# Float64 weight words without a clamp, the split of w_out in the first up stage, and output stores on SyncE's queue, in a RetNet and SwiGLU kernel

## The chip, the cores and the metric

The kernel runs on one core of one Trainium2 chip. The metric is the device time in microseconds (us); lower is better. The engines are named PE (TensorE), ACT (ScalarE), DVE (VectorE), POOL (GpSimd) and SP (SyncE, which only issues transfers here).

## The reference

Retention over 4 sequences of 768 tokens with 8 heads of 64, then a gated feed-forward block on the 3072 x 512 result.

```python
for t in range(S):
    state = gamma * state + outer(k[t], v[t])      # per batch and head, 64 x 64
    y[t] = (1 / sqrt(D)) * q[t] @ state
x = y as (3072, 512)
g = x @ w_gate                                      # 512 x 1536
out = (g * sigmoid(g) * (x @ w_val)) @ w_out        # 1536 x 512
```

q, k and v are float32. The three weight matrices arrive as float64; the kernel gets them as 64-bit words and makes float32 of them itself.

## The kernel before, in words

**Segments.** The 24 chunks of 128 tokens are worked in four segments (NSEG) of six chunks, three each of two sequences. A segment has an attention part, an *up stage* (gate and value products for 12 slices of 128 columns of d_ff, f = 0 to 11) and a *down stage* (out += h[f] @ w_out[f], six token blocks in six PSUM banks). The attention of the next segment is woven into a down stage.

**The first segment is different.** Its up stage (`up`, L591) uses float32 products, seven per f (a seven-product scheme for the 2 x 2 blocks of x and the weights, `product` L599, matmul at L601, 28 matmuls per f). Later segments (`up3`, L769) use three passes of rounded parts per product (matmul at L765), and every down stage does so too (`down`, L829, matmul at L832). The parts are made by `near_a/b/c` (L657 to L664) and `far_a/b/c/d` (L666 to L676): a rounded leading part on ACT, a remainder on DVE or POOL, and a combination; `far` has a fourth operation, a scaling on ACT.

**Weights in the first up stage.** A *piece* is one slice f of gate and value ("up", 128 x 1024 words) or of w_out ("down", 128 x 512 words). Pieces 0 to 11 are up, 12 to 23 are down. A piece is loaded as raw 64-bit words (`load_piece`, letters U and D), and converted:
- `convert_a` on ACT: part a takes the absolute value of the high words as float (L219), part b copies the high words into a PSUM bank to keep the sign (L223), part c scales the low words and adds an offset (L226).
- `convert_b` on DVE: letter B clamps to a minimum and maximum (L236) and shifts left by 3 (L238), letter S takes the sign bit out of the PSUM copy and puts it in (L242), in parts of 512.
- `convert_c` on POOL (letter C, L252) adds the two as integers.

An up piece then gets three sums on DVE (`sums_t`, letter T, L266 through L80) and is stored in DRAM (`w_up`) for the later segments. A down piece is stored as plain float32 (`w_dn`, L203).

**The split of w_out** is in segment 0's down stage (`w_load`, L807): each slice is loaded from `w_dn` into chunk_x, split in three (`far_a` ACT L667, `far_b` POOL L670, `far_c` DVE L673, `far_d` ACT L676) into a tile `oitem` (three slots), used, and stored to `w_dn3`. Later segments only load `w_dn3`, 8.0 ahead of the use in the planner's time.

**What sets the order.** Each engine works in the order of issue. In the first up stage the order is written out: `aside(f, place)` runs the letters in the table `beside[f, place]` between the products of a step, place 0 to 5; in the text such a place is also counted as q = 6 f + place. Transfers to DRAM wait in `stores` until two places later. Everything else is put in a list of events with a due time in us of an assumed plan (`at`, L121), and `run` issues those due. In the plan a step of the first up stage takes UP0 = 9.45 and starts from T0 = 18. All loads, and the stores of weights, are issued from SP. `up` copies the first product of a step to `p1` on ACT (L620) before the bank is used again; `up3` does so with L781, which is issued through the helper line L122.

**The end of a down stage.** `finish` (L836) brings a bank out with ACT (even blocks, L845) or DVE (odd blocks, L843) into chunk_x, and issues the store of the output from ACT (L846).

**Side tables.** `load_side` brings turned decay tables for the later segments over the tables of the prologue, and `load_pair` loads k, q, v of the next segment; in the first up stage both come near the end.

Of the kernel before, what the change touches and what calls it, by code (L numbers as in the profile page):

```python
# [49 lines left out]
def tile_retnet_swiglu(  # L50
# [42 lines left out]
    spare = [place(f"spare{i}", 3 * DM, tag=f"o{i}") for i in range(3)]  # L93
# [61 lines left out]
    w_dn = [kept.tile([P, DM], F32, name=f"wdn{f}", tag=f"wdn{f}") for f in range(NF)]  # L155
# [16 lines left out]
    def load_piece(piece):  # L172
# [24 lines left out]
        if not wide and kind == "down":  # L197
            keep_dn(piece)

    def keep_dn(piece):  # L200
        kind, a = piece
        if kind == "down":
            nc.sync.dma_start(out=w_dn[a], in_=made[a % 5])  # L203
# [9 lines left out]

    def convert_a(piece, own, part=None):

        if piece in raw:
            d, lo, hi = words_of(piece)
            if part in (0, None):
                nc.scalar.activation(d, hi.bitcast(F32), AF.Abs)  # L219
            if part in (1, None):  # L220
                signs[piece] = []
                for i, o in enumerate(own):
                    nc.scalar.copy(banks[o], hi[:, ts(i, 512)].bitcast(F32))  # L223
                    signs[piece].append(banks[o])
            if part in (2, None):
                nc.scalar.activation(lo.bitcast(F32), lo, AF.Copy, scale=2.0 ** -51,  # L226
                                     bias=2.0)

    def convert_b(piece, part=None):


        if piece in raw:
            d = words_of(piece)[0]
            u = d.bitcast(U32)
            if part in (0, None):
                nc.vector.tensor_scalar(d, d, 122879.9921875, 2.0 ** -15, op0=ALU.min,  # L236
                                        op1=ALU.max)
                nc.vector.tensor_scalar(u, u, 3, None, op0=ALU.logical_shift_left)  # L238
            if part in (1, None):
                for i, t in enumerate(signs.pop(piece)):  # L240
                    v = u[:, ts(i, 512)]
                    nc.vector.scalar_tensor_tensor(v, t.bitcast(U32), 0x80000000, v,  # L242
                                                   op0=ALU.bitwise_and,
                                                   op1=ALU.bitwise_xor)


    def convert_c(piece, halves=1):
        if piece in raw:
# [6 lines left out]
            stores.append((places[0], lambda: keep_dn(piece)))  # L255
# [14 lines left out]
    pieces = [("up", f) for f in range(NF)] + [("down", f) for f in range(NF)]  # L270
# [767 lines left out]
```

## Time and profile before

| what | value |
|---|---|
| runs | 705.17, 706.85, 814.71 us; median 706.85 |
| profiled run | 704.16 us, span of instructions 702.4 us, mean granted clock 0.989 |
| PE, DVE, ACT, POOL busy | 95%, 71%, 56%, 35% of the span |
| data moved | 140.8 MB, mean 200 GB/s |
| first product of the first up stage to first down matmul | 29.69 to 145.26 us |
| down stage 0, first matmul to the first of segment 1's up stage | 145.26 to 230.72 us |
| the same for segment 1 and segment 2 | 321.09 to 391.88, 484.54 to 555.47 us |
| last down stage to the end | 648.9 to 702.4 us |

Times of operations are from one profiled execution. A group's mean is the length of one instruction; two of them on ACT or DVE that follow each other start about 0.1 us less than that apart. The busy time of PE counts overlapping matmuls once and is modelled at the ends, so distances between starts are the better measure for PE.

### The profile page before, as it was taken

The page shows a single profiled execution, that of the slowest core. Times are in us where ns is not written, and L with a number is a line of the kernel's source. Part 1 is how long each engine was busy: PE and PEld are TensorE (multiplying, and loading weights), DVE is VectorE, ACT ScalarE, POOL GpSimd, SP SyncE. Part 2 cuts the span into 40 slices and gives each one's busy share as a digit, 9 for nine tenths or more (in the row PEclk, how much of TensorE's full clock was granted, in tenths as well). Part 3 has the DMA queues.
Part 4 walks back from the last instruction along what each step waited for, and adds up shares of the span by engine and source line. Part 5 has one row for each costly group of instructions (what it writes and reads, how often), then busy time and mean ns, then how long its engine had stood idle before and what let it go on. Part 6 is the DMA issues. An engine that isn't in the chain of part 4 may idle for free.

```text
span 702.4 us, 12451 instructions
## 1 busy us (share of the span) xinstructions
PE 664.6 (95%) x4724; PEld 552.3 (79%) x4724; DVE 496.8 (71%) x778; ACT 391.4 (56%) x805; POOL 247.9 (35%) x164
## 2 busy tenths in 40 slices
PE   7998999998888999999999899999999899999997
PEld 6754555566666899997767899998777699999886
DVE  3887988796898666675677766766577856767641
ACT  2658687628757555454478555555464555554211
POOL 0434443441322566550101565661011355553000
PEclk9999999999999999999999999999999999999999
DMA  8796699876567534174766443354656553322554
GB/s 314 259 378 229 213 378 400 282 228 223 185 233 253 196 108 156 59 234 173 250 203 210 180 138 125 105 185 153 224 184 217 209 187 107 123 88 90 190 208 142
DMA packets 51740, 140.81 MB, mean 200 GB/s; under 512 B 6368, under 2 KB 19168, under 8 KB 51680
## 3 DMA queue, kind: packets, MB, share of 16 engines
q1 hardware_dynamic: 48224, 133.72, 55.2%
q10 hardware_dynamic: 3456, 6.29, 2.5%
q8 instruction: 37, 0.61, 0.3%
q14 instruction: 23, 0.19, 0.1%
HBM read 110.11 MB, written 29.88 MB: 199 GB/s over the span
## 4 chain that ended last, share of the span: by engine, by line
PE 63%; DVE 16%; ACT 8%; DMA 6%; issue 4%; SPq 1%; POOL 0%; ACTq 0%; DVEq 0%; POOLq 0%
PE bank L765 35%; PE bank L832 15%; PE bank L601 9%; PE bank L458 4%; DVE gitem L661 3%; ACT chunk_x L696 3%; DVE x L673 2%; DVE x L80 2%; ACT gitem L658 2%; DVE gitem L80 1%; DVE tmp L80 1%; DMA loads<-in_v_n_dram 1%; DVE tmp L477 1%; DVE first L80 1%; DMA rawp<-in_q_t_dram 1%
## 5 line engine op out<-in xcount | busy, mean ns | idle before, releaser
L765 PE MATMUL bank<-x,gitem 128*128 128x384 f32 x1296 | 235.4, 338 | 7.5 <-ACT tmp L122 7.5
L765 PEld LDWEIGHTS bank<-x,gitem 128*128 128x128 f32 x1296 | 228.0, 190 | 9.8 <-ACT tmp L122 9.4
L832 PE MATMUL bank<-oitem,gitem 128*128 128x512 f32 x864 | 213.7, 401 | 4.2 <-ACT oitem L676 2.9
L832 PEld LDWEIGHTS bank<-oitem,gitem 128*128 128x128 f32 x864 | 160.7, 190 | 43.2 <-issue 4.5
L664 POOL TENSOR_TENSOR gitem<-gitem 128x768 fp32r<-128x768 f32 x72 | 135.6, 1883 | 128.0 <-DVE gitem L661 128.0
L661 DVE SCALAR_TENSOR_TENSOR gitem<-gitem,loads 128x768 fp32r<-128x768 f32 x72 | 74.0, 1027 | 68.2 <-ACT gitem L658 68.2
L601 PE MATMUL bank<-first 128*128 128x384 f32 x336 | 111.6, 490 | 2.7 <-DVE hT L636 1.6
L601 PEld LDWEIGHTS bank<-first 128*128 128x128 f32 x336 | 62.7, 190 | 49.7 <-DVE hT L636 2.4
L661 DVE SCALAR_TENSOR_TENSOR gitem<-gitem,hT 128x768 fp32r<-128x768 f32 x48 | 47.9, 997 | 48.0 <-ACT gitem L658 48.0
L658 ACT ACTIVATE gitem<-loads 128x768 fp32r<-128x768 f32 x72 | 60.8, 845 | 3.1 <-DVE oitem L661 3.1
L252 POOL TENSOR_TENSOR first<-first,rawp 128x1024 int32<-128x1024 int32 (+1 forms) x21 | 39.9, 1915 | 58.9 <-DVE first L242 21.9
L122 ACT ACTIVATE bank<-bank 128x384 f32<-128x384 f32 x36 | 17.1, 475 | 75.1 <-PE bank L765 75.1
L658 ACT ACTIVATE gitem<-hT 128x768 fp32r<-128x768 f32 x48 | 39.8, 837 | 25.0 <-PE bank L832 24.8
L122 ACT COPY tmp<-bank 128x384 f32<-128x384 f32 x108 | 50.9, 473 | 4.0 <-PE bank L765 4.0
L531 POOL TENSOR_TENSOR loads<-loads,tab 128x512 f32<-128x512 f32 x8 | 13.8, 1729 | 110.9 <-PE bank L458 110.9
L80 DVE SCALAR_TENSOR_TENSOR gitem<-gitem 128x768 fp32r<-128x768 f32 x48 | 51.4, 1072 | 1.0
L122 DVE TENSOR_TENSOR hT<-bank,tmp 128x384 f32<-128x384 f32 x72 | 39.8, 555 | 17.1 <-PE bank L765 16.5
L765 PE MATMUL bank<-x,oitem 128*128 128x384 f32 x216 | 44.3, 340 | 0.4 <-DVE hT L122 0.4
L122 DVE TENSOR_TENSOR hT<-hT,bank 128x384 f32<-128x384 f32 x72 | 39.8, 553 | 5.1 <-ACT bank L122 1.5
L122 ACT ACTIVATE bank<-tmp 128x384 f32<-128x384 f32 x36 | 17.9, 496 | 43.8 <-DVE tmp L122 43.8
L696 ACT COPY chunk_x<-bank 64x256 f32<-64x256 f32 x72 | 26.4, 366 | 24.2 <-PE bank L458 22.7
L765 PEld LDWEIGHTS bank<-x,oitem 128*128 128x128 f32 x216 | 36.9, 187 | 2.4 <-DVE hT L122 1.6
(97 smaller groups left out, 694.8 us busy)
## 6 DMA issues: line engine op xcount, KB each, us to landing
loads<-wup SPq DMA_DIRECT2D x36, 896.0 KB, 4.6
oitem<-wdnt SPq DMA_DIRECT2D x36, 768.0 KB, 4.4
wup<-first SPq DMA_DIRECT2D x12, 896.0 KB, 8.5
wdnt<-oitem SPq DMA_DIRECT2D x12, 768.0 KB, 4.3
rawp<-in_w_val_dram SPq DMA_DIRECT2D x24, 256.0 KB, 5.6
rawp<-in_w_gate_dram SPq DMA_DIRECT2D x12, 512.0 KB, 6.8
out_dram<-chunk_x ACTq DMA_DIRECT2D x24, 256.0 KB, 2.1
loads<-in_k_t_dram SPq DMA_DIRECT2D x18, 256.0 KB, 3.6
```

The costliest lines, as they stand in the source:

```text
L80: stt(o, x, 1.0, y, op0=mul, op1=op)
L122: events.append((t, len(events), lambda: fn(*args, **kw)))
L252: pool(d[:, ts(i, n)].bitcast(I32), d[:, ts(i, n)].bitcast(I32), lo[:, ts(i, n)].bitcast(I32), op=add)
L458: nc.tensor.matmul(o, a, b, start=start, stop=True, skip_group_check=True)
L601: nc.tensor.matmul(o, w[:, slot, k], a[:, k], start=(start and k == 0), stop=(stop and k == KH - 1), skip_group_check=True)
L658: act(o[0], x, AF.Copy, scale=CUT / FAR)
L661: stt(o[1], f32(o[0]), -FAR, x, op0=mul, op1=add)
L664: op(o[2], f32(o[0]), f32(o[1]), op=add)
L673: stt(o[2], f32(o[0]), 1.0 / FAR, f32(o[1]), op0=mul, op1=sub)
L696: copy(cx[half[i], ds(2 * h, 2), c], y_both(h, i, c))
L765: nc.tensor.matmul(o, w[:, a, k], xs_of[s][:, a, OP[p], k], start=start and a == k == 0, stop=a == 2 and k == KH - 1, skip_group_check=True)
L832: nc.tensor.matmul(banks[tok], hs[f][:, a, ds(i * TH + u * P, P)], wo[f][:, a], start=f == a == 0, stop=f == NF - 1 and a == 2, skip_group ...
```

## The change

1. *Conversion without a clamp.* Part a is a Copy with a scale instead of the absolute value and keeps the sign. Part b is a parametric ReLU (`Prelu`) of the result of part a, written as an integer to the PSUM bank, instead of a copy of the high words. Part c is a scaled Copy written as an integer. The clamp and the shift (letter B) are gone: S is now a single operation of DVE per 512 that shifts left by 3 and ORs the bank in.
2. *The split of w_out moved.* `three_dn` (letter F, parts 0 to 3) makes the three parts of each slice in the first up stage and stores them to `w_dn3`; `w_dn` is gone. The down pieces come in the order f = 3 to 11, 0, 1, 2, so that the last three stay in the three `oitem` slots; in segment 0's down stage `w_load` loads the others from `w_dn3`, with the same lead as in later segments. A table gives the place q of every part of every piece, and of the loads. Raw down words go to `loads` instead of `spare` tiles.
3. *Stores of the output* are issued from SP instead of ACT.
4. *Moved beside that:* `load_side` in four parts with fewer transfers, and the five `load_pair`, spread over the second half of the first up stage; `k4 t4 k5 t5` (the scaling and state products of the last two chunks) from steps 9 to 11 to steps 3 to 5.

```diff
             if part in (0, None):
-                nc.scalar.activation(d, hi.bitcast(F32), AF.Abs)
+                act(d, hi.bitcast(F32), AF.Copy, scale=2.0 ** -112)
...
-                    nc.scalar.copy(banks[o], hi[:, ts(i, 512)].bitcast(F32))
+                    act(banks[o].bitcast(I32), d[:, ts(i, 512)], AF.Prelu, scale=2.0 ** 94,
+                        alpha=2.0 ** 127)
...
-                nc.scalar.activation(lo.bitcast(F32), lo, AF.Copy, scale=2.0 ** -51,
-                                     bias=2.0)
+                act(lo.bitcast(I32), lo, AF.Copy, scale=2.0 ** -29)
...
-                nc.vector.tensor_scalar(d, d, 122879.9921875, 2.0 ** -15, op0=ALU.min,
-                                        op1=ALU.max)
-                nc.vector.tensor_scalar(u, u, 3, None, op0=ALU.logical_shift_left)
...
-                    nc.vector.scalar_tensor_tensor(v, t.bitcast(U32), 0x80000000, v,
-                                                   op0=ALU.bitwise_and,
-                                                   op1=ALU.bitwise_xor)
+                stt(u[:, ts(i, 512)], u[:, ts(i, 512)], 3, t.bitcast(U32),
+                    op0=ALU.logical_shift_left, op1=ALU.bitwise_or)
...
-            stores.append((places[0], lambda: keep_dn(piece)))
+
+    def three_dn(piece, part):
+        a = piece[1]
+        if part == 0:
+            wo[a] = item("o", DM)
+        o, x = [wo[a][:, i] for i in range(3)], made[a % 5]
+        if part == 0:
+            far_a(o, x)
+        elif part == 1:
+            far_b(o, x, pool)
+        elif part == 2:
+            far_c(o)
+        else:
+            far_d(o)
+            stores.append((places[0], lambda: nc.sync.dma_start(
+                out=w_dn3[a], in_=wo[a].bitcast(U32))))
...
+    DOWN = [*range(3, NF), 0, 1, 2]
+    pieces = [("up", f) for f in range(NF)] + [("down", f) for f in DOWN]
...
+    when = [(12, 9, 10, 10, 11, 11, 16, 19, 20), (4, 13, 14, 14, 15, 15)]
+    when += [(f + 2, 6 * f - 3, 6 * f - 2, 6 * f - 1, 6 * f + 1, 6 * f + 1) for f in range(3, 10)]
+    when += [(f + 11, *(6 * f + i for i in (1, 1, 2, 3, 3, 5, 8, 9))) for f in range(2, 11)]
+    when += [(22, 63, 63, 64, 64, 64, 66, 67, 68), (23, 67, 67, 68, 68, 68, 69, 70, 71)]
+    loads_at = [(11, "D"), (15, "U")] + [(6 * f + 1, "U") for f in range(3, 7)]
+    loads_at += [(6 * f + 3, "D") for f in range(2, 10)] + [(50, "D")]
...
+        parts_of = "abcSC" if n < NF else ["a", "b", "c", "S", "C", "F", "F", "F"]
...
-    beside[9, 5] = "k4 k5"
-    beside[10, 3] = "t4"
-    beside[11, 3] = "t5"
+    beside[3, 5] += " k4"
+    beside[4, 4] += " t4 k5"
+    beside[5, 4] += " t5"
...
-        at(t - (24.0 if f < 2 else 11.5), lambda: nc.sync.dma_start(out=raw_w, in_=w_dn[f]))
-        t -= 3.0 * (f < 2)
-        at(t - 7.3, begin)
-        at(t - 6.5, lambda: far_b([wo[f][:, i] for i in range(3)], raw_w, pool))
-        at(t - 4.5, lambda: far_c([wo[f][:, i] for i in range(3)]))
-        at(t - 3.5, lambda: far_d([wo[f][:, i] for i in range(3)]))
-        at(t + 1.0, lambda: nc.sync.dma_start(out=w_dn3[f], in_=wo[f].bitcast(U32)))
...
-        nc.scalar.dma_start(out=out[ds(row, P)], in_=t)
+        nc.sync.dma_start(out=out[ds(row, P)], in_=t)
...
-            w_load(steps[f], s, f)
+            if s or f > 2:
+                w_load(steps[f], f)
...
-    at(T0 + 30, load_side, 0)
-    at(end - 11, load_side, 1)
+    for i in range(4):
+        at(T0 + UP0 * (6.2 + i / 2), load_side, i // 2, i % 2)
     for n in range(5):
-        at(end - 20 + 2 * n, load_pair, 1, n)
+        at(T0 + UP0 * (7.4, 8.4, 9.2, 10.2, 10.8)[n], load_pair, 1, n)
```

## The prediction

> **What bounds the kernel now.** I read in this order: busy times by stage, groups with shapes kept apart, TensorE (PE) in order of time, ScalarE (ACT) in order of time where PE waits.
>
> The first view gives one line per stretch: 30 to 145 is the first up stage, the others are the down stages of segments 0, 1 and 2. Columns: PE, PE's weight loads, VectorE (DVE), ACT, GpSimd (POOL), each with its count, then granted clock, DMA share, GB/s.
>
> ```profile
> 30.00:145.00 115.00, 110.87 (x364) 62.82 (x362) 99.53 (x178) 84.18 (x143) 48.36 (x28) 1.00 0.85 301
> 145.00:230.00 85.00, 73.05 (x761) 55.34 (x762) 71.49 (x97) 52.80 (x119) 22.70 (x15) 0.96 0.64 223
> 322.00:395.00 73.00, 70.33 (x769) 54.62 (x767) 52.90 (x79) 45.61 (x114) 8.88 (x5) 1.00 0.60 205
> 486.00:561.00 75.00, 69.43 (x768) 54.33 (x767) 53.49 (x81) 41.75 (x98) 10.73 (x6) 1.00 0.61 203
> ```
>
> Segment 0's down stage has the same PE work as segment 2's (about 760 matmul records each), yet takes some 10 us more, with DVE 18 us, ACT 11 us and POOL 12 us busier and the clock at 0.96. The first up stage has every engine heavily loaded: DVE 99.5 of 115 us, ACT 84.2, DMA 0.85 of its 16 engines.
>
> The second view names the extra work (mean ns, then idle time before):
>
> ```profile
> L670 POOL TENSOR_TENSOR oitem<-oitem,chunk_x 128x512 fp32r<-128x512 f32 x12 | 18.4, 1532 | 54.9 <-ACT oitem L667 43.0 <-DVE x L80 6.8 <-issue 5.0
> ...
> L238 DVE TENSOR_SCALAR first<-first 128x1024 uint32<-128x1024 uint32 x12 | 10.4, 868 | 0.4
> ...
> L673 DVE SCALAR_TENSOR_TENSOR oitem<-oitem 128x512 fp32r<-128x512 f32 x12 | 9.3, 771 | 2.1 <-POOL oitem L670 2.1
> ...
> L236 DVE TENSOR_SCALAR first<-first 128x1024 f32<-128x1024 f32 x12 | 8.2, 687 | 1.3 <-ACT first L219 1.3
> ...
> L676 ACT ACTIVATE oitem<-oitem 128x512 fp32r<-128x512 f32 x12 | 7.5, 625 | 23.0 <-DVE oitem L673 23.0
> L667 ACT ACTIVATE oitem<-chunk_x 128x512 fp32r<-128x512 f32 x12 | 7.4, 617 | 0.0
> ```
>
> The four `oitem` groups with 12 calls are the splitting of w_out, only in segment 0's down stage; the two L236/L238 groups are half of the clamp and shift (the 512-wide halves take 420 and 427 ns).
>
> The third view is PE in time: the first up stage,
>
> ```profile
> 29.69 1.56 PE L601 MATMUL bank<-first 128*128 128x384 f32 x4
> ...
> 60.20 2.85 PE L601 MATMUL bank<-first 128*128 128x384 f32 x8 [1.56 <-DVE hT L636]
> 63.53 66.74 PE L601 MATMUL bank<-first 128*128 128x384 f32 x204 [0.48 <-ACT tmp L620]
> ...
> 145.26 0.73 PE L832 MATMUL bank<-oitem,gitem 128*128 128x512 f32 x2 [0.35 <-DVE hT L617]
> ```
>
> and the first and third down stage's ends:
>
> ```profile
> 230.72 2.25 PE L765 MATMUL bank<-x,gitem 128*128 128x384 f32 x12
> 233.81 4.47 PE L765 MATMUL bank<-x,gitem 128*128 128x384 f32 x24 [0.84 <-ACT tmp L122]
> ```
>
> ```profile
> 484.54 1.55 PE L832 MATMUL bank<-oitem,gitem 128*128 128x512 f32 x6
> ...
> 555.47 2.26 PE L765 MATMUL bank<-x,gitem 128*128 128x384 f32 x12
> 561.00 5.80 PE L765 MATMUL bank<-x,gitem 128*128 128x384 f32 x24 [3.26 <-ACT tmp L122]
> ```
>
> Between 63.53 and 130.3 PE issues 204 products without a hole: 66.6/204 = 0.326 us each. The whole stage has 332 before 145.26, 108.4 us, plus two `state` steps of about 0.6: a floor of 109.6 in a stage of 145.26 - 29.69 = 115.6. So 6 us are holes, and counts by start times place them: the 24 products before 38.54 take 1.0 us more than 24 x 0.326, the 68 from there to 63.53 take 2.8 more, 1.5 are lost between 130.1 and `state` at 131.6, 0.6 at the end. A down stage from its first matmul to the next stage's first is 230.72 - 145.26 = 85.5 us for segment 0, and 555.47 - 484.54 = 70.9 for segment 2. PE then stands 3.26 us for an ACT copy. The last view says why:
>
> ```profile
> 555.42 0.60 ACT L845 ACTIVATE chunk_x<-bank 128x512 f32<-128x512 f32 x1
> 556.05 0.34 ACTq L846 DMA_DIRECT2D out_dram<-chunk_x  x1
> 556.43 0.42 ACT L658 ACTIVATE oitem<-loads 128x256 fp32r<-128x256 f32 x1 [0.41 <-ACT chunk_x L845]
> 557.46 0.34 ACTq L846 DMA_DIRECT2D out_dram<-chunk_x  x1
> 557.84 0.60 ACT L845 ACTIVATE chunk_x<-bank 128x512 f32<-128x512 f32 x1 [0.99 <-PE bank L765]
> 558.47 1.16 ACTq L846 DMA_DIRECT2D out_dram<-chunk_x  x2
> 559.73 0.84 ACT L658 ACTIVATE gitem<-loads 128x768 fp32r<-128x768 f32 x1 [1.29 <-DVE oitem L661]
> 560.48 0.46 ACT L122 COPY tmp<-bank 128x384 f32<-128x384 f32 x1
> ```
>
> ACT issues the output stores (ACTq) in its own stream; each store of an odd token waits there for DVE's chunk_x, and the copy of `p1` that frees PE stands behind all of them. The same hole is 2.20 us at 396.35 and 0.84 us at 233.81.
>
> **What the Trainium skill says.** (1) "SBUF — State Buffer", section "SBUF: two separate sides": DVE and GpSimd share one port pair as an exclusive lock; a DVE operation in a two-port mode or with two SBUF inputs takes it, and the other blocks. The trace agrees: the shift L238 took 2.78 us at 44.22 beside a POOL add running 43.72 to 46.45, against 0.69 undisturbed (33.87); the L80 sum at 185.29 took 1.91 us beside L670 on POOL, against 0.95 without. The clamp and shift removed are such operations; the sign step has one operand in PSUM and is not. (2) "DMA: Bandwidth & Descriptors", "Issuing engines are not separate DMA queues": a store from SP or ACT runs on the same 16 engines; only the issuer's time is saved. The trace has that time: 0.34 us each, plus waits. (3) "ScalarE: Activation LUTs", "Table sets: the hidden batching unit": cheap functions lie in every set, a function outside the active set costs a load. It doesn't say in which sets the parametric ReLU lies. The trace has one load, 1283 ns, at the start, for Silu.
>
> **The change part by part**, against the span of 702.4 us.
>
> *Conversion.* Removed: 12 x (687 + 868) + 12 x (420 + 427) ns = 28.8 us of DVE (25.6 by start-to-start distances), all in the prologue and the first up stage, and with it the port clashes. The sign step stays 36 calls of 682 ns, with in1 instead of in0 in PSUM: no change. On ACT, Abs becomes a scaled Copy of the same shape (1169 and 679 ns), the offset copy stays (1171, 695), and the 36 copies to PSUM (633) become Prelu of the same size. Prelu isn't in the trace; between 540 ns (the distance at which such copies follow each other) and 633 plus a table load of 1283 each way. I take 633, no load. New: Prelu reads what the Copy before it wrote, so the overlap of about 0.09 us is lost, 24 times, 2 us of ACT.
>
> *Splitting moved.* Per piece ACT 617 + 625, POOL 1532, DVE 771 ns leave the down stage and enter the up stage: 14.9, 18.4 and 9.3 us. Also gone there: 12 loads of raw w_out and 12 stores; 9 loads of 768 KB come in their place, with the same lead of 8.0 as in later segments, where they cause no hole. What remains is segment 2's stage: 70.9, plus the last gates (4 products, 1.3 us), plus about 1.0 us to fill. 85.5 - 73.2 = 12.3 us less. Bounds: 8 if the attention chain of this segment (hole of 2.80 us at 172.43 on `states`) has its own cause; 13.
>
> *First up stage.* Per step of 28 products (9.14 us) ACT needs, by distances between starts, 1.95 (three copies, two Silu) + 3.24 (up piece) + 1.70 (w_out piece) = 6.9 us; with the split's 1.05 and the lost overlap 8.1, still below 9.14. DVE: 99.5 - 28 + 9 = about 81 of 112 us, and perhaps 11 us of clashes with twelve further POOL operations. POOL: 48 + 18 = 66. DMA: 34.6 MB - 3.1 - 0.8 (raw w_out out and back) + 9.4 = about 40 MB in 112 us = 359 GB/s; the stretch 91 to 120 moved 407 GB/s with PE busy 28.91 of 29.0 us, so this fits, with little left. The 2.8 us end at DVE's L636 (60.20) and ACT's L620 (63.53): the sum waits behind clamp, shift and sign of piece 4, the `p1` copy behind the conversions of pieces 5 and 12. Clamp and shift (1.3 us) go, piece 12 is converted a step earlier where ACT sits idle (3.35 us before 49.65): 2.0 of it saved. `k4 k5 t4 t5` move to steps 3 to 5, where they cost PE the same 0.6 us each; I take the wait of 1.5 as gone, and 0.5 of the first hole. 4 us less in all. Bounds: 5 less; 6 more, if in-order waiting on far_b (POOL), far_c (DVE), far_d (ACT) stalls the bank copies. Behind each far_d stand the bank copies that PE waits for; the order gives POOL and DVE three places (3.9 us) for far_b and one (1.3 us) for far_c. Side tables and chunk loads leave the end of the stage for its middle: SP issues of 0.4 to 0.6 us each, hidden by a whole step (9 us) or more between a load and its use.
>
> *Stores on SP.* 24 x 0.34 us and their waits leave ACT. Behind them on SP stands only load_unit(3), due 12 us later (it is issued at 559.09 and has to wait anyway). Holes: 0.84 + 2.20 + 3.26 = 6.3 us; the operation ahead of the copy (L658 at 559.73) is also said to wait for DVE's `oitem` until 559.06, so not all is ACTq's. I take half, 3.0 us (0.5 to 6). At the kernel's end the chain runs matmul, eviction, store, landing as before: 0.
>
> Sum: 702.4 - 12.3 - 4.0 - 3.0 = 683.1 us of span. The median of the runs, 706.85, is 4.45 above this span (the profiled run itself took 704.16), so 687.5 us.
>
> **The rivals.**
> - *The up stage gives a part back* (0.12). For: ACT at 8.1 of 9.14 us per step with in-order waits, POOL and DVE clashing. Against: DVE loses three times what it gains. With 0.8 us lost in each of ten steps the stage is 4 longer instead of 4 shorter: 695.5.
> - *The down stage was long for another reason* (0.08): the attention chain and DMA landings, clock 0.96. For: the `states` and `loads` waits in its chain. Against: segment 2 has the same chain without the holes. With 4 of 12.3 us gained: 695.8.
> - *DMA becomes the bound of the up stage* (0.05). The stretch 60 to 80 moved 244 GB/s at a share of 0.72, so 339 at full share; 40 MB take 118 us at that, 6.4 more than taken: 694.
> - *Slower: Prelu needs a table of its own* (0.05). Each up step then has two switches, Silu to Prelu and back. At the 1283 ns of the trace ACT needs 10.7 us per step, at the 2.66 us that the skill's ACT_TABLE_LOAD section gives (load and drain) 13.4 instead of 9.14: 4.2 us over, ten steps, 42 us: 729. It decides for slower above about 2.2 us per switch. For it: nothing in the trace. Against: the skill's cheap functions in every set.
> - That the change doesn't do what it says isn't likely: the clamp's instructions are plainly gone.
>
> **How the numbers follow.** The first case has 0.70, its own range 680 to 693; 2% (about what can be told from no change here) lies at 692.7. Faster: 0.66 of it, 0.04 each of the first two rivals: 0.74. Slower: 0.05, the table. Same: 0.21. The range 679 to 700 takes in the first three rivals and leaves out the table and the tails.
>
> **What would show it.** In the profile after: no L236/L238 groups; the split's groups before 145 us; no ACTq stores; first down matmul to first up matmul of segment 1 about 73 us; up stage about 111.6; holes at the two later changes of stage about half. More than one table load, an up stage above 118, or a first down stage above 78 would make it wrong.

## The result and the profile after

The median of four runs is 696.04 us (695.74 to 696.65) beside 706.22 us for the kernel before: a ratio of 0.986, with a 95% interval from 0.984 to 0.988. One of the four runs of the kernel before took 814.71 us; the ratio leaves it out, and the median of the others is 705.59 us. The profiled span is 693.9 us instead of 702.4. The kernel is 1.4% faster, which is clear of the noise and inside the forecast range of 679 to 700, but under the 2% that the forecast asked of "faster". It ends 8.5 us above the forecast of 687.5, and the stage that the change works on most became longer instead of shorter.

The stages, each from its first matmul to the first of the next (us, from PE in order of time; "up" is the products, "down" the products with w_out):

| | first product at | up 0 | down 0 | up 1 | down 1 | up 2 | down 2 | up 3 | down 3 | span |
|---|---|---|---|---|---|---|---|---|---|---|
| before | 29.69 | 115.57 | 85.46 | 90.37 | 70.79 | 92.66 | 70.93 | 93.43 | 53.50 | 702.4 |
| after | 29.35 | 121.35 | 73.37 | 90.98 | 71.47 | 90.08 | 71.60 | 90.84 | 54.86 | 693.9 |
| difference | -0.34 | +5.78 | -12.09 | +0.61 | +0.68 | -2.58 | +0.67 | -2.59 | +1.36 | -8.5 |

Four things can be read from this table: the first down stage lost what was forecast; the first up stage, forecast 4 us shorter, became 5.8 longer; the up stages 2 and 3, which begin with the holes of the output stores, lost 2.6 us each; and every down stage without a split became 0.7 us longer, the last one 1.4 us, which no step of the forecast had.

The windows of the kernel after, the same stretches as before (PE, weight loads, DVE, ACT, POOL, clock, DMA share, GB/s):

```profile
30.00:145.00 115.00, 107.04 (x351) 60.12 (x349) 81.51 (x137) 87.90 (x154) 58.52 (x35) 1.00 0.89 316
145.00:230.00 85.00, 81.68 (x802) 61.45 (x803) 63.19 (x95) 50.67 (x116) 16.89 (x10) 0.98 0.62 225
322.00:395.00 73.00, 70.60 (x718) 55.12 (x719) 54.10 (x81) 44.40 (x104) 13.57 (x7) 1.00 0.59 206
486.00:561.00 75.00, 71.62 (x729) 56.59 (x729) 55.05 (x83) 41.57 (x91) 15.13 (x9) 1.00 0.62 211
```

DVE fell from 99.5 to 81.5 us in the first up stage, as worked out. POOL, ACT and the DMA engines rose, and the stretch 145 to 230, with DVE 8 us lower, is now closer to those of the later segments. So the work is where it was forecast to be; still PE did 107 us of its work in that stretch instead of 111. PE in order of time says where it stood:

```profile
29.35 1.56 PE L604 MATMUL bank<-first 128*128 128x384 f32 x4
...
63.38 13.91 PE L604 MATMUL bank<-first 128*128 128x384 f32 x40 [0.97 <-ACT tmp L623]
77.90 0.69 PE L399 MATMUL bank<-kept_vk 128*64 128x64 f32 x16 [0.60 <-issue]
...
89.69 0.69 PE L399 MATMUL bank<-chunk_x 128*64 128x64 f32 x16 [1.56 <-issue]
90.30 51.90 PE L604 MATMUL bank<-first 128*128 128x384 f32 x160
145.42 4.77 PE L604 MATMUL bank<-first 128*128 128x384 f32 x9 [3.22 <-ACT tmp L628]
```

From 63.5 to 130 the kernel before had one group of 204 products without a hole. In the kernel after there are holes of 0.97, 0.60 and 1.56 us before 90.30, then 160 products without one (0.32 us each, as before), and then one of 3.22 us at 145.42, released by ACT's copy L628. The sum of the holes that this view marks between 29 and 151 us is 8.3 us, beside 4.3 us in the kernel before. Most of what is left of the 5.8 us is the clock: for 3.41 us from 145.26 on, the granted clock is 0.50, and the products behind the hole start 0.64 us apart instead of 0.32, some 1.6 us in all. The window there has 0.83 in the column of the clock:

```profile
140.00:150.00 10.00, 6.78 (x16) 3.51 (x15) 3.62 (x7) 5.43 (x11) 2.92 (x3) 0.83 1.02 401
```

PE of the kernel after at the last change of stage, where it stood 3.26 us before:

```profile
548.20 4.50 PE L768 MATMUL bank<-x,gitem 128*128 128x384 f32 x24
553.80 2.42 PE L768 MATMUL bank<-x,gitem 128*128 128x384 f32 x12 [1.10 <-ACT tmp L121]
```

ACT at the same place:

```profile
547.80 0.60 ACT L833 ACTIVATE chunk_x<-bank 128x512 f32<-128x512 f32 x1
548.29 0.41 ACT L661 ACTIVATE oitem<-loads 128x256 fp32r<-128x256 f32 x1
548.60 0.59 ACT L833 ACTIVATE chunk_x<-bank 128x512 f32<-128x512 f32 x1
549.08 0.84 ACT L661 ACTIVATE gitem<-loads 128x768 fp32r<-128x768 f32 x1
549.82 0.48 ACT L121 COPY tmp<-bank 128x384 f32<-128x384 f32 x1
552.85 0.49 ACT L121 ACTIVATE bank<-tmp 128x384 f32<-128x384 f32 x1 [2.55 <-DVE tmp L121]
553.28 0.47 ACT L121 COPY tmp<-bank 128x384 f32<-128x384 f32 x1
```

ACT goes from one eviction (L833) to the next and to the copy of `p1` (L121 at 549.82) with no store (ACTq) and no wait between them, and PE runs on: its 24 products from 548.20 have no hole, where the kernel before stood 3.26 us after the first 12. The hole of 1.10 us at 553.80 is another one. It ends with the second copy of the stage (553.28), which stands behind a Silu (552.85) that waits 2.55 us for a sum of DVE. The two changes of stage before this one show the same: the holes of 0.84 and 2.20 us at the first copy are gone, and holes of 1.04 us (229.60) and 0.58 us (391.44) stand at the second. The three changes together have 2.7 us of such holes instead of 6.3.

The clock changed with them. In the kernel before, two stretches of 3.41 us at a granted clock of 0.50 begin at 396.73 and 560.57, at the holes of 2.20 and 3.26 us, and PE's products start 0.32 us apart in them instead of 0.17. The kernel after has no such stretch at its changes of stage. The window of the kernel before inside the second:

```profile
560.60:563.90 3.30, 2.90 (x9) 2.90 (x10) 1.43 (x2) 1.42 (x4) 1.82 (x1) 0.50 0.84 304
```

The groups of the kernel after with shapes kept apart (mean ns as the second number after the bar) have the one new function and the clash of ports:

```profile
L216 ACT ACTIVATE bank<-first 128x512 int32<-128x512 f32 x36 | 20.5, 593 | 0.4
...
L676 DVE SCALAR_TENSOR_TENSOR oitem<-oitem 128x512 fp32r<-128x512 f32 x12 | 12.5, 1051 | 13.1 <-POOL oitem L673 13.1
```

L216 is Prelu: 593 ns, against 633 for the copy that it replaced; one table load of 1283 ns remains in the whole trace, as before. L676 is `far_c`, which took 771 ns in the down stage. Its mean of 1051 mixes two cases: ten of the twelve take 676 to 694 ns, and two take 2.87 us, at 84.72 and 122.60, each begun just after an integer sum of POOL (L235):

```profile
84.72 2.87 DVE L676 SCALAR_TENSOR_TENSOR oitem<-oitem 128x512 fp32r<-128x512 f32 x1 [1.35 <-POOL oitem L673]
...
84.65 2.40 POOL L235 TENSOR_TENSOR first<-first,rawp 128x1024 int32<-128x1024 int32 x1
```

This is the DVE and GpSimd lock of the Trainium skill ("SBUF — State Buffer", section "SBUF: two separate sides"), by which whichever of the two starts first keeps the other waiting, in its new place: 3.4 us of DVE more than in the down stage.

### The profile page after: what moved, and what is told of

Same layout as the page of the kernel before. It is cut to its first block, busy times and chain, and to the rows that moved or that the text cites. A ratio compares the mean times of both kernels' runs of the same rounds, so it can differ in the third digit from the quotient of the medians.

```text
span 693.9 us, 12332 instructions
## 1 busy us (share of the span) xinstructions
PE 666.2 (96%) x4724; PEld 548.7 (79%) x4724; DVE 466.0 (67%) x730; ACT 389.2 (56%) x805; POOL 250.3 (36%) x164
## 4 chain that ended last, share of the span: by engine, by line
PE 62%; DVE 16%; ACT 9%; DMA 8%; issue 4%; SPq 1%; POOL 0%; DVEq 0%; ACTq 0%; POOLq 0%
PE bank L768 34%; PE bank L820 14%; PE bank L604 10%; PE bank L461 4%; ACT chunk_x L699 4%; DVE gitem L664 3%; DVE x L676 2%; DVE x L80 2%; DMA rawp<-in_w_gate_dram 2%; DMA wdnt<-oitem 1%; DVE tmp L80 1%; DVE gitem L80 1%; DMA loads<-in_q_t_dram 1%; ACT gitem L661 1%; DVE chunk_x L831 1%
## 5 line engine op out<-in xcount | busy, mean ns | idle before, releaser
L768 PEld LDWEIGHTS bank<-x,gitem 128*128 128x128 f32 x1296 | 225.6, 188 | 6.9 <-ACT tmp L121 6.2
L820 PEld LDWEIGHTS bank<-oitem,gitem 128*128 128x128 f32 x864 | 158.8, 188 | 40.6 <-issue 3.3
L604 PE MATMUL bank<-first 128*128 128x384 f32 x336 | 113.7, 496 | 6.2 <-ACT tmp L628 3.9
L664 DVE SCALAR_TENSOR_TENSOR gitem<-gitem,hT 128x768 fp32r<-128x768 f32 x48 | 46.3, 964 | 47.2 <-ACT gitem L661 46.8
L121 ACT ACTIVATE bank<-bank 128x384 f32<-128x384 f32 x36 | 17.1, 475 | 78.6 <-PE bank L768 78.6
L235 POOL TENSOR_TENSOR first<-first,rawp 128x1024 int32<-128x1024 int32 (+1 forms) x21 | 41.1, 1961 | 39.5 <-DVE first L226 12.1
L121 ACT COPY tmp<-bank 128x384 f32<-128x384 f32 x108 | 51.2, 476 | 2.1 <-PE bank L768 2.1
L121 DVE TENSOR_TENSOR hT<-bank,tmp 128x384 f32<-128x384 f32 x72 | 39.6, 553 | 16.7 <-PE bank L768 16.7
L80 DVE SCALAR_TENSOR_TENSOR gitem<-gitem 128x768 fp32r<-128x768 f32 x48 | 45.8, 955 | 1.0
L121 ACT ACTIVATE bank<-tmp 128x384 f32<-128x384 f32 x36 | 17.8, 496 | 48.2 <-DVE tmp L121 48.2
L121 DVE TENSOR_TENSOR hT<-hT,bank 128x384 f32<-128x384 f32 x72 | 39.9, 554 | 4.9 <-ACT bank L121 1.6
L679 ACT ACTIVATE x<-x 128x512 fp32r<-128x512 f32 (+2 forms) x27 | 18.9, 700 | 37.8 <-DVE x L676 37.8
```

Source lines behind the costliest of these rows:

```text
L80: stt(o, x, 1.0, y, op0=mul, op1=op)
L121: events.append((t, len(events), lambda: fn(*args, **kw)))
L235: pool(d[:, ts(i, n)].bitcast(I32), d[:, ts(i, n)].bitcast(I32), lo[:, ts(i, n)].bitcast(I32), op=add)
L604: nc.tensor.matmul(o, w[:, slot, k], a[:, k], start=(start and k == 0), stop=(stop and k == KH - 1), skip_group_check=True)
L664: stt(o[1], f32(o[0]), -FAR, x, op0=mul, op1=add)
L679: act(o[2], f32(o[2]), AF.Copy, scale=FAR / ONE)
```

## The experiments

Two questions were open: what lengthened the first up stage, and what lengthens the down matmuls. For the first, the trace offered this chain. SP's queue of the kernel after, in order of time:

```profile
100.04 0.72 SPq L439 DMA_DIRECT2D tab<-in_decays_dram  x1
105.59 1.26 SPq L441 DMA_DIRECT2D tab<-in_decays_dram  x2
...
114.41 1.25 SPq L441 DMA_DIRECT2D tab<-in_decays_dram  x2
...
116.40 0.53 SPq L252 DMA_DIRECT2D wdnt<-oitem  x1
...
134.57 0.33 SPq L252 DMA_DIRECT2D wdnt<-oitem  x1
```

SP issues L439 at 100.04 and its next transfer, L441, only at 105.59. The new `load_side` writes 2P columns for both i in one transfer (L439), and the second writes beside it into the same tile. The list of waits names the releaser of L441 as the landing of the first transfer (9.5 us in all, two times, longest 4.8). It happens again with the next L439, issued at 108.65, before 114.41. The same pair of transfers into `kept_vk` (117.03 and 122.51), of the same shape, doesn't wait, so the shape alone isn't the reason; why `tab` differs stays open. In the kernel before, whose tables for `tab` came earlier than described above and one i at a time, ten such transfers go out between 72.80 and 81.08 and none waits for another. Everything behind stands too: loads of raw words and the stores of split pieces (L252), of which the next goes out at 116.40 and the last shown at 134.57. The windows of 10 us of the same kernel show it from the other side (DMA share and GB/s at the end):

```profile
100.00:110.00 10.00, 10.00 (x32) 5.89 (x31) 6.74 (x14) 9.01 (x18) 6.50 (x4) 1.00 0.57 184
110.00:120.00 10.00, 10.00 (x32) 5.89 (x31) 7.47 (x14) 9.02 (x16) 5.54 (x4) 1.00 0.63 198
120.00:130.00 10.00, 10.00 (x32) 5.89 (x31) 9.43 (x15) 5.25 (x11) 4.91 (x3) 1.00 1.00 343
```

A share of 0.57 and 0.63 for 20 us, then 1.00: work that was not issued, made up at the limit. The stores land late. ACT of the kernel after, in order of time:

```profile
130.32 0.63 ACT L670 ACTIVATE oitem<-first 128x512 fp32r<-128x512 f32 x1 [4.19 <-DMA wdnt<-oitem]
...
144.37 0.63 ACT L670 ACTIVATE oitem<-first 128x512 fp32r<-128x512 f32 x1 [3.84 <-DMA wdnt<-oitem]
144.91 0.46 ACT L628 COPY tmp<-bank 128x384 f32<-128x384 f32 x1
```

`far_a` (L670) needs a free `oitem` slot, which is free when its store (`wdnt<-oitem`) has landed. It stood 4.19 us at 130.32 and 3.84 us at 144.37; behind the second is the copy L628 that releases PE's hole of 3.22 us.

**Side tables in transfers of one i each** (the one transfer for both i becomes one for each i):

```diff
-        nc.sync.dma_start(out=side[g][half[m], :, : 2 * P], in_=cols[half[0]])
         for i in range(2):
+            nc.sync.dma_start(out=side[g][half[m], i, : 2 * P], in_=cols[half[0], i])
             nc.sync.dma_start(
```

> The changed kernel with the first part of each side table loaded by one DMA for each half i, as before, instead of one DMA for both. In the changed kernel SP stands twice for 4.8 us, from 100.7 and 109.6, ahead of the second DMA, which is said to wait for the first to land; DMA is idle meanwhile (shares 0.57 and 0.63 in 100 to 120), then at 1.0 until 150; the stores of split w_out go out late, a far_a on ACT waits 4.19 and 3.84 us for its slot, and PE stands 3.2 us behind it. Theory A, the overlap wait of the side tables is the start of it: the two SP waits go, the PE hole at 142 to 145 goes or shrinks to under 1 us, the up stage (first product to first down matmul) falls from 121.4 to 116 to 118, the total by 3 to 5 us to 691 to 693. Theory B, DMA bandwidth is the bound: the work only moves, the up stage stays within 1.5 us. Theory C, ACT's own load is the bound: no change either, and ACT waits for nothing but PE.

691.69 us (ratio to before 0.980, 0.975 to 0.985), 4.3 less than the kernel after; the first up stage 117.56 us, 3.8 less. The windows of this kernel:

```profile
100.00:110.00 10.00, 10.00 (x33) 5.89 (x32) 7.41 (x15) 9.02 (x16) 5.67 (x4) 1.00 0.87 281
110.00:120.00 10.00, 10.00 (x33) 5.89 (x32) 6.85 (x13) 9.02 (x17) 6.48 (x4) 1.00 0.95 287
...
140.00:150.00 10.00, 9.18 (x29) 5.02 (x28) 5.76 (x10) 6.34 (x12) 4.91 (x4) 1.00 0.83 338
```

The share is 0.87 and 0.95 where it was 0.57 and 0.63, and SP has no gap at L441. PE:

```profile
91.43 53.16 PE L604 MATMUL bank<-first 128*128 128x384 f32 x164
144.92 2.85 PE L604 MATMUL bank<-first 128*128 128x384 f32 x8 [0.34 <-ACT tmp L631]
```

164 products run through, and the end of the stage has a hole of 0.34 us instead of 3.22. The clock from 140 to 150 is 1.00 instead of 0.83, which is some 1.6 of the 3.8 us. The chain is shown: two waits of SP made the late stores, and these the hole. One of the waits for an `oitem` slot is left on ACT in this kernel:

```profile
83.84 0.63 ACT L670 ACTIVATE oitem<-first 128x512 fp32r<-128x512 f32 x1 [3.66 <-DMA wdnt<-oitem]
```

**The last part of the split on DVE instead of ACT** (on top of the edit above), since ACT was the busiest engine of the stage after PE, with the bank copies behind `far_d`:

```diff
-            far_d(o)
+            nc.vector.tensor_scalar(o[2], f32(o[2]), FAR / ONE, None, op0=mul)
```

> The run with the side tables split (691.7), and in the first up stage the last operation of the split (far_d, a scaling) on DVE instead of ACT: 12 operations of about 0.63 us less on ACT, 12 of about 0.43 more on DVE. In the run with the side tables split the stage is still 117.6 against a floor near 108.7, and the holes are put down to ACT bank copies. Theory A, ACT's in-order stream is what is left: the stage falls by 1.5 to 3 us, the total to 689 to 690. Theory B, what is left is the chain of POOL, DVE and slot waits: no change within 0.7 us.

693.83 us (0.983, 0.982 to 0.985): 2.1 slower than without it, the up stage 118.81. PE's new hole in this kernel:

```profile
62.48 5.65 PE L604 MATMUL bank<-first 128*128 128x384 f32 x16 [0.99 <-ACT tmp L623]
70.80 9.67 PE L604 MATMUL bank<-first 128*128 128x384 f32 x24 [2.67 <-DVE hT L620]
```

PE waits 2.67 us for DVE's hT (L620), and the granted clock is 0.50 for 3.41 us from 71.19 on. The hole of 0.99 us at ACT's copy L623 is still there, with 7.5 us of work taken from ACT. Of the later holes, the one of 0.58 us at 84.89 is gone and the wait of 1.56 us at 90.81 is 0.39. So `far_d` on ACT doesn't make the hole of 0.99 us, and what it costs ACT elsewhere is less than what it costs on DVE.

**Parts alone: only the conversion, on the kernel before** (the split in the down stage and the stores on ACT stay):

```diff
-                nc.scalar.activation(d, hi.bitcast(F32), AF.Abs)
+                act(d, hi.bitcast(F32), AF.Copy, scale=2.0 ** -112)
...
-                    nc.scalar.copy(banks[o], hi[:, ts(i, 512)].bitcast(F32))
+                    act(banks[o].bitcast(I32), d[:, ts(i, 512)], AF.Prelu, scale=2.0 ** 94,
+                        alpha=2.0 ** 127)
```

> The kernel before with the conversion of the change alone: scaled Copy, Prelu to the bank, scaled Copy; no clamp, one shift-and-or per 512 on DVE; the split of w_out stays in down stage 0, the stores on ACT. Theory A, the conversion is worth time by itself: the holes of the first up stage at 56.7 to 63.5 were DVE's clamp and shift, the stage falls from 115.6 by 1.5 to 3 us and the total by as much, to 702. Theory B, in the old order DVE was not what PE waited for, the conversion only makes room for the moved split: the time stays within 1 us of the kernel before.

701.85 us (0.994, 0.992 to 0.996), and a first up stage of 111.59. PE in it:

```profile
31.62 29.48 PE L596 MATMUL bank<-first 128*128 128x384 f32 x88 [0.37 <-DVE first L80]
61.64 66.06 PE L596 MATMUL bank<-first 128*128 128x384 f32 x204 [0.55 <-ACT tmp L615]
```

88 and 204 products without a hole: the stage has the length that the forecast gave to the whole change (111.6). That the two agree so closely is luck, since the forecast's 4 us counted on the new order of work as well: the wait of the state products, for one, is gone here in their old place. The conversion's 4 us are there; the rest of the change uses them up.

**The opposite: the old conversion in the new order of work** (Abs, Copy, clamp, shift and sign back in their places):

```diff
-                act(d, hi.bitcast(F32), AF.Copy, scale=2.0 ** -112)
+                act(d, hi.bitcast(F32), AF.Abs)
...
+            nc.vector.tensor_scalar(d, d, 122879.9921875, 2.0 ** -15, op0=ALU.min, op1=ALU.max)
+            nc.vector.tensor_scalar(u, u, 3, None, op0=ALU.logical_shift_left)
```

> The changed kernel with the conversion of before in its order of today: absolute value, copy of the high words to the bank, offset copy; clamp, shift and sign together where S stands. Theory A, the clamp-free conversion makes the room on DVE that the moved split needs: DVE gets some 25 us more in the first up stage (busy 81.5 to about 107 of the 115 us from 30 to 145) and clashes with POOL again, the stage grows from 121.4 by 4 us or more, the total to 700 or more. Theory B, the room was not needed, ACT's order alone makes the holes: the stage stays within 1.5 us of 121.4 and the total within 1.5 of 696.

714.66 us (1.014, 1.011 to 1.017): 18.6 more than the kernel after, 16.1 of it in the first up stage (137.44). PE in it:

```profile
67.10 11.84 PE L606 MATMUL bank<-first 128*128 128x384 f32 x28 [6.23 <-DVE hT L641]
...
90.87 1.12 PE L401 MATMUL bank<-kept_vk 128*64 128x64 f32 x16 [4.60 <-issue]
```

PE waits 6.23 us for DVE's hT at 67.10, and 4.60 us at 90.87, where the view names no releaser. At each of the two the granted clock is 0.50 for 6.83 us, some 5 us of lower clock in this stage, where the kernel after has 1.6. DVE is busy for 102 of the 115 us from 30 to 145 instead of 81.5. Without the new conversion DVE can't take the split in this order of work: the same edit is worth 4 us alone and 16 us with the split beside it.

**The stores: only they go back to ACT in the kernel after, and only they go to SP in the kernel before.**

```diff
-        nc.sync.dma_start(out=out[ds(row, P)], in_=t)
+        nc.scalar.dma_start(out=out[ds(row, P)], in_=t)
```

> The changed kernel with the output stores issued from ACT again. Theory A, the stores on SP are worth the holes at the changes of stage: the up stages of segments 2 and 3 (first product to first down matmul) grow from 90.1 and 90.8 to about 92.7 and 93.4, the first from 91.0 to about 91, the total grows by 4 to 6 us to 700 to 702. Theory B, the gain there came from elsewhere (fewer operations queued on DVE or ACT): total within 1 us of 696.

> The kernel before with its output stores issued from SP, nothing else. Undoing this part in the changed kernel cost 6.3 us. Theory A, the part is additive: the kernel before falls by 4.5 to 6.5 us, to 698.5 to 700.5 beside 704.9, from the up stages of segments 1 to 3. Theory B, it pays only with the split moved away, since the down stage 0 of before has its own stores of w_out on SP: under 3 us.

Back on ACT: 702.24 us (0.996, 0.995 to 0.998), 6.2 more than the kernel after. PE of this kernel at the last change of stage has its hole back:

```profile
557.32 5.89 PE L768 MATMUL bank<-x,gitem 128*128 128x384 f32 x24 [2.55 <-ACT tmp L121]
```

Alone on the kernel before: 699.0 us (0.990, 0.988 to 0.992), 6.8 less. Single traces show less than the medians: up stages 1 to 3 together are 4.6 us shorter in the kernel after than in the kernel before, 5.2 shorter than with the stores back on ACT, and 4.1 shorter with only the stores on SP than in the kernel before. The traces also show that a hole costs more than its length. With the stores back on ACT, the holes of 2.58 us (229.98) and 2.55 us (557.32) each come with a stretch of 3.41 us at a granted clock of 0.50; the one of 1.88 us (393.80) has none. By the times that PE works in these stretches, the clock is some 3.0 us of the difference and the holes 3.3, together a little more than the whole.

More of such stretches may be what the medians have beyond the traces. The mean granted clock is 0.992 in the median of the runs with the stores back on ACT, and 0.995 to 0.998 in those of the kernel after; it is 0.987 in the median of the kernel before, and 0.993 to 0.995 with its stores on SP. No run changes the clock alone, so this is not shown.

**The place of the `oitem` tiles.** In the last down stage PE runs nothing but down matmuls. In the kernel before 216 of them took 49.16 us (start to start 0.2267 us). PE of the kernel before and of the kernel after in that stage:

```profile
648.90 49.16 PE L832 MATMUL bank<-oitem,gitem 128*128 128x512 f32 x216
...
639.04 50.56 PE L820 MATMUL bank<-oitem,gitem 128*128 128x512 f32 x216
```

0.2333 us each, in every slice, though clock and instructions are the same. Besides data, only addresses changed: without the `spare` tiles the three `oitem` tiles moved from byte 154752 of each partition to 210656. Four kernels move them and change no instruction (tiles declared behind a new line move along, but these matmuls read none of those): `spare` back where it was; 32 bytes added to `warm`, so that they start at a multiple of 64 (210688); a line after `tmp` (187520); a line after `chunk_x` (195712, so that the last of them ends at 214144, above the start of those of the kernel after).

```diff
     rawp = [place(f"rawp{i}", 3 * 2 * TH, tag=f"g{i}") for i in range(4)]
+    spare = [place(f"spare{i}", 3 * DM, tag=f"o{i}") for i in range(3)]
...
-    warm = place("warm", P + 1)
+    warm = place("warm", P + 9)[:, : P + 1]
```

> The changed kernel with the three spare tiles of before declared again but not used, which puts every tile back at the address it had before. Theory A (alignment) and C (place): 216 matmuls of the last down stage in about 49.2 us instead of 50.6, and the total at about 691. Theory B (chip or execution): 50.6 as in the changed kernel.

> The changed kernel with 32 more bytes per partition in front of the oitem tiles, nothing else. In the changed kernel every down-stage matmul takes 0.234 us (216 in 50.6 us in the last stage) against 0.228 before (49.2). There the oitem tiles, which these matmuls stream, start at byte 210656 of a partition, a multiple of 32 and not of 64; before they started at 154752, a multiple of 64. Theory A, the start address decides: the last down stage falls back to about 49.2 us, each of the four by 1.3, the total by 4 to 5.5 us, to about 691. Theory B, it is the chip or the execution: the rate stays 0.234 and the time 696; or both kernels show the same rate on this chip. Theory C, place in memory but not this alignment: stays at 0.234 here and falls in the run with the old layout.

> The changed kernel with the oitem tiles between tmp and chunk_x: they start at 187520, 193664 and 199808, all multiples of 64, where 154752 gave 0.2267 us per down matmul in the last stage, 210656 gave 0.2333 and 210688 gave 0.2323. Theory A, only addresses above some bound are slow: 0.2267 for all or for the first slot, slower for the others, so that the mean per slice f repeats with period 3. Theory B, it is the position relative to other tiles, the granules of the address or the like: one rate for all slices.

> The changed kernel with the oitem tiles behind chunk_x, at 195712, 201856 and 208000, all 128 above a multiple of 512 as were the places with 0.2267 us per matmul (154752, 187520); the slow ones lay 224 and 256 above one. Theory A, a high region is slow: the third slot, which ends at 214144, is slower, so the mean per slice repeats with period 3, up to 0.233 for every third. Theory B, the offset within a granule decides: 0.2267 for all slices.

PE in the last down stage with `spare` back:

```profile
637.07 49.16 PE L821 MATMUL bank<-oitem,gitem 128*128 128x512 f32 x216
```

| `oitem` starts at | start to start, us | 216 matmuls, us | kernel, us |
|---|---|---|---|
| 154752 (`spare` back) | 0.2267 | 49.16 | 692.42, one run |
| 187520 | 0.2267 | 49.16 | 694.57, one run |
| 195712 | 0.2267 | 49.16 | 695.58, one run |
| 210656 (after) | 0.2333 | 50.56 | 696.04 |
| 210688 | 0.2323 | 50.34 | 695.88 |

That the place decides is shown. It isn't alignment to 64 bytes (210688 has it and is slow), nor the upper region as such: from 195712 on all three slots are fast, the last of them up to byte 214144, while in the kernel after the first third of the first slot, 210656 to 212704, is slow (0.231 us). The three fast places all lie 128 above a multiple of 512, the two slow ones 224 and 256 above one. But the fast places lie 32768 and 8192 bytes apart, so they agree in every smaller power of two as well; which property of the address it is stays open. With `spare` back the four down stages are 0.57, 0.58, 0.65 and 1.33 us shorter, 3.1 us; the kernel, in one run, 3.6. The two other fast places show less in the whole time, and their first product came later in these runs (30.76 and 31.42 us instead of 29.35).

**Together.** First the side tables apart and `spare` back. Then also four loads of up pieces two thirds of a step later, because in the kernel with the side tables apart the store for the slot at 83.84 was behind one of those loads on SP, which had to wait for POOL until 70.7 and so let the store go only at 73.66.

```diff
-    loads_at = [(11, "D"), (15, "U")] + [(6 * f + 1, "U") for f in range(3, 7)]
+    loads_at = [(11, "D"), (15, "U")] + [(6 * f + 5, "U") for f in range(3, 7)]
```

> The changed kernel with the side tables' first part loaded by one DMA per half (alone: 696.0 to 691.7 us) and the oitem tiles back at their old address (alone: 692.4). Theory A, the two are separate costs of the change, one of SP's order and one of the place of a tile, and add up: 696.0 - 4.3 - 3.6 = 688.1, the up stage at 117 to 118, the last down stage at 53.5. Theory B, they overlap: 690 to 691.

> The kernel of the run above with the up pieces 8 to 11 loaded four places later (6 f + 5 instead of 6 f + 1). With the side tables split, one slot wait is left: far_a on ACT waits 3.66 us until 83.8 for a store of w_out that SP issued at 73.7 only, since the load of an up piece ahead of it on SP waited for POOL to free its buffer until 70.7. Theory A, that in-order wait on SP is the cause: the stores of w_out go out 4 us or more earlier, the wait falls under 1 us, the up stage falls by 1 to 2.5 us. Theory B, the DMA queue is full there in any case: the wait stays, or the later pieces come late and the stage does not fall.

689.04 us (0.979, 0.976 to 0.982) and 687.55 us (0.976, 0.974 to 0.979). The second is the fastest kernel of this study. Its store is issued at 67.27, `far_a` waits for no slot any more, and its first up stage is 115.29 us. PE in it:

```profile
63.64 13.93 PE L605 MATMUL bank<-first 128*128 128x384 f32 x40 [0.99 <-ACT tmp L624]
78.15 0.69 PE L400 MATMUL bank<-kept_vk 128*64 128x64 f32 x16 [0.59 <-issue]
...
88.12 0.69 PE L400 MATMUL bank<-chunk_x 128*64 128x64 f32 x16
88.74 53.16 PE L605 MATMUL bank<-first 128*128 128x384 f32 x164
```

What is left is short holes, at copies on ACT mostly and nearly all before 90 us, some 4 us in all. Taking `far_d` from ACT left the largest, 0.99 us, as it was; what else orders them was not tried.

## Why the prediction was right and wrong

- **The number** is in the forecast range, but outside the range of its first case (680 to 693). "Faster", by 2%, had been given 0.74 and did not come; "same", which came, 0.21. The forecast's own sign of being wrong, an up stage above 118 us, came (121.35). The range held because it was wide, and because errors went against each other: the span is 10.8 us above the forecast of 683.1, the stores gave 1.6 more than forecast, and the 4.45 us added from the span to the median are only 2.1 in the kernel after.
- **Down stage 0**: 73.2 us forecast, 73.37 measured, 12.1 us less instead of 12.3. Some 3.4 of the 12.1 are the clock: the kernel before has two stretches of 3.41 us at 0.50 in this stage (from 185.11 and 226.06), the kernel after none. Reading the stage of a later segment, whose clock is 1.00, as what remains was right; the rival that the attention chain is long for its own reason is refuted.
- **The conversion**: 4 us less in the up stage, shown by the kernel with it alone (115.57 to 111.59). Clamp and shift gone, DVE at 81 us, Prelu with no table load (593 ns, within the 540 to 633 taken): all as forecast, and the rival that ends slower is refuted.
- **The moved split in the first up stage is the step that failed.** The forecast said of side tables and chunk loads "SP issues of 0.4 to 0.6 us each, hidden by a whole step (9 us) or more between a load and its use". It counted the issues of SP and not their waits: that one transfer into a tile can stand behind another, and what is queued behind them on SP. The runs showed two waits of 4.8 us, 20 us of DMA engines at a share of about 0.6, stores that give `oitem` slots back too late, 11.4 us of ACT's waits for these slots, and a hole of 3.22 us with 1.6 us of lower clock behind it; taking the two waits away gives back 3.8 us. The forecast followed the `oitem` slots nowhere. A second term: "I take the wait of 1.5 as gone" for the state products; they kept it (1.56 at 89.69), in their new place, until the up loads went later, while the conversion alone takes it away in their old place. Of the rest above 111.6, 2.3 us went with `spare` back and the later loads (117.56 to 115.29); 3.7 stay, about the sum of the short holes that are left, and what orders these is not settled.
- **The rival "the up stage gives a part back"** had the direction, and its time (695.5) is nearly the measured one. Its mechanism was only half right: in-order waiting on ACT, yes, but at `far_a` for a slot, not at `far_b`, `far_c` or `far_d` for another engine, and the time has the slower matmuls in it, which the rival hadn't. **DMA as the bound** is refuted as it was stated: with the side tables apart the engines are as full from 120 us on (1.04 in 120 to 130), and PE runs through; and the last kernel moves the same bytes in a stage of 115.29 us, under the 118 that this rival asked for.
- **Stores on SP**: 3.0 us forecast, 4.6 in the up stages of the trace and 6.2 to 6.8 us in the medians of the runs. The holes at the first copy went wholly, not by half, and smaller ones at the second copy came in their place; 6.3 us became 2.7, so "I take half" was near in size for another reason. The term that was put at nothing is the clock, some 3 us in these stages.
- **The rate of the down matmuls**, 3.1 us, was in no step: that raw down words go to `loads` instead of `spare` tiles was given no cost, and the change of addresses that comes with it was not seen.

The forecast's sum, corrected by what the trace showed: -12.1 in down stage 0 (its slower matmuls included), -4.0 by the conversion and +9.8 by everything else in the first up stage, -4.6 in the other up stages, +2.7 in the other down stages, -0.3 for an earlier first product: -8.5, as measured. Parts alone give the same picture: the conversion by itself is worth 3.8 us and the stores by themselves 6.8. What the moved split adds, with the moves of part 4, can be read from two kernels that both have the new conversion and their stores on ACT: 702.24 us with the split moved (0.996 of the kernel before), 701.85 us without (0.994). The moved split, the largest single gain of the forecast, was worth nothing net as it was written; with the three repairs the total is 16.6 us (704.1 to 687.55).

## What to carry to other kernels

Work moved into a fuller stage brings its transfers along: follow every buffer slot that it takes to the transfer that gives it back, and read on the issuing queue what stands before that transfer, waits included and not only the time to issue. Two transfers into one tile can wait for each other (here a pair whose ranges interleave did in one tile and not in another); a gap between two issues of the queue, with a DMA share that falls and then stays at its limit, is how it looks. When a hole of PE comes or goes, read the granted clock just behind it too: the hole can cost more than its length. When tiles are added or removed, compare the start-to-start distance of an instruction that did not change: the addresses did.

## What the runs showed of the hardware

- The rate of an fp32r 128x512 matmul follows the place of its streamed tile: 0.2267 us at 154752, 187520 and 195712 bytes, 0.2333 and 0.2323 at 210656 and 210688, 2.5 to 2.9% apart with no instruction changed.
- The granted clock fell to 0.50 around holes of PE. Between the first product and 690 us the fourteen traces have 23 holes of more than 2 us; at 17 of them a stretch of 3.41 us at 0.50 (6.83 at the two longest) begins within 1.7 us of the hole's end, and six have none. There is one further such stretch, at 185.11 in the kernel before, after a hole of 1.50 us. The three traces without a hole of this length there have none. In a stretch, products of 128x384 start 0.32 us apart instead of 0.17, or 0.64 instead of 0.32 in the first up stage, so that one costs up to 1.7 us.
- Output stores moved off ACT's queue were worth 6.2 to 6.8 us in the medians, for 24 issues of mostly 0.34 us (some 8 us), though ACT is busy only 56% of the span: the holes of PE behind them went, and the lower clock at these holes.
- A conversion that takes 26 to 29 us off DVE is worth 4 us alone and 16 us when another 9 us of DVE work is put beside it: what a freed engine is worth depends on what is waiting for it.
